# FFN2's operand sums taken from accumulating DMA to VectorE, in a kernel whose whole order is written out by hand

## The chip, the cores and the metric

The kernel runs on one core of a Trainium2 chip. The metric is device time in microseconds, as a median of several executions. A core has engines that work side by side, each through its own queue in order: TensorE (PE; its weight loads stand apart as PEld), VectorE (DVE), ScalarE (ACT), GpSimd (POOL) and SyncE (SP). DMA transfers are issued by POOL (its queue also casts and accumulates), SP and ACT.

## The reference, cut to what matters

```python
k_all = concat([beacon_k, k]); v_all = concat([beacon_v, v])      # 16 beacon rows, then S = 576
scores = scale * q @ k_all.T                                       # causal mask on the 576, none on the 16
a = softmax(scores); attn = a @ v_all                              # B = 8, H = 8, D = 64
x = attn as [4608, 512]
h = x @ w_in                                                       # 512 -> 2048
g = where(h > 0, h, exp(min(h, 0)) - 1)                            # ELU
out = g @ w_out                                                    # 2048 -> 512
```

## The kernel before, in words

Attention goes by batch b (0 to 7), each with two head groups of four; the two-layer feed-forward network goes by token tile t. Tiles 0 and 1 are two halves of the first 512 tokens, tiles 2 to 9 have 512 tokens each. The work of different batches and tiles is interleaved, so attention of a later batch fills engines while the network works on an earlier tile. Attention ends inside tile 7; tiles 8 and 9 run alone.

**The order is a list of words**, run from top to bottom by `run` (L825): `Q.6.0.7` calls step `Q` with 6, 0, 7. Each engine gets its instructions in the order of this list and does them in that order; between engines only data and buffers make anything wait. A last letter `v` puts a step on DVE that ACT does otherwise (`u`, `U`, `J`, `K`); `d`, in `Z` and `D`, made it an accumulating DMA. The steps that this text uses:

- `S`: scores of one column group on PE; `x`: their exponential on ACT; `m`: the causal mask on DVE; `D`: sums of exponentials on DVE; `L`, `W`: row sums and weighted values on PE; `n`, `M`: the normalisation.
- FFN1 of tiles 0 to 5: `F` on PE into one of the `hps` banks (pool of two), `e` (exponential, ACT), `u` (relu, ACT or DVE), `k` (DVE: joins them into the operand `gt`). `r` and `g` are another way of the same on DVE.
- FFN1 of tiles 6 to 9 is done by seven block products instead of eight: `X` and `H` make operand sums on DVE, `P` multiplies (4 matmuls), `K` copies a partial result (ACT, or DVE with `v`) or adds one (DVE), `E`, `U`, `V` are the exponential, the relu and the join.
- FFN2, also by seven products of blocks: `wt` makes the weight sums once, `Z.t.n` makes the operand's block sums for tile t, `Q.t.a.b` does matmuls a to b of the tile's 112, `J.t.p` takes a finished product out of PSUM (ACT, or DVE with `v`) and issues the store. Stores of tiles 3 to 8 accumulate in HBM.
- `lq`, `lk`, `lt`, `lp`, `lv`, `wi`, `wo`: loads; `lk`, `lv` and the weights are issued by POOL, the transposes `lt` by SP. `warm`: matmuls of zeros at the start.

`Z.t.n` works in place on the blocks A of `gt`: n = 3 writes A00 - A01 to its own tile `s3`; n = 1 adds A11 to A01; n = 2 makes A00 = A01 - A00; n = 4 takes A00 from A10. `B` is the whole tile, 0 or 1 a half (both only for tile 9). n = 2 reads what n = 1 wrote. The products of `Q` follow the order of `PH`: matmuls 0 to 31 read blocks before these sums, from 32 on those after n = 2, from 48 on n = 1's.

Of the six sums `Z.3.1` to `Z.8.1` the kernel before makes a DMA on POOL's queue (L571):

```python
nc.gpsimd.dma_start(out=o_, in_=b_, accum_op=op_)
```

All other `Z`, `H` and `wt` are a `tensor_tensor` on DVE (L573).

Of the kernel before, what the change touches and what calls it, by code (L numbers as in the profile page):

```python
# [12 lines left out]
ALU = mybir.AluOpType  # L13
# [4 lines left out]
def kernel(  # L18
# [107 lines left out]
    for b in range(BD):  # L126
        o_ = 0
# [62 lines left out]
    op = {}  # L190
# [378 lines left out]
    def sub(o_, a_, b_, op_=ALU.subtract, eng="v"):  # L569
        if eng == "d":  # L570
            nc.gpsimd.dma_start(out=o_, in_=b_, accum_op=op_)  # L571
            return
        (nc.vector if eng == "v" else nc.gpsimd).tensor_tensor(out=o_, in0=a_, in1=b_, op=op_)  # L573
# [258 lines left out]
    warm.1 lq.0.0.0.4 warm.1 warm.1 lq.0.1.0.4 warm.4 warm.1 lq.0.0.4.8 warm.1 warm.4 ident  # L832
    warm.1 bt bk T.0.0.0 cb.0.1 warm.1 cb.0.0 cb.0.2 warm.1 ck.0.0.0 lq.0.1.4.8 T.0.1.0 S.0.0.0
    T.0.0.1 cq.0.1.0 S.0.1.0 x.0.0.0 warm.1 cq.0.0.1 T.0.1.1 S.0.0.3 x.0.1.0 T.0.3.0 S.0.0.2
    cq.0.1.1 x.0.0.3 T.0.2.0 cq.0.3.0 lq.1.0.0.4 x.0.0.2 S.0.1.3 x.0.1.3 cb.0.3 warm.1 S.0.1.1
    x.0.1.1 T.0.2.1 S.0.1.2 tri cb.1.1 m.0.0.3 warm.1 x.0.1.2 S.0.3.0 cq.0.2.0 cq.0.2.1 T.0.3.1
    S.0.2.3 lv.0.2 warm.1 lv.0.0.1 x.0.3.0 m.0.3.0 m.0.0.0 x.0.2.3 S.0.2.0 m.0.1.0 x.0.2.0
    m.0.2.0 S.0.0.1 x.0.0.1 wi.2 S.0.2.2 x.0.2.2 L.0.A cb.1.0 T.1.0.0 cq.1.0.0 T.1.1.0 n.0.A
    cq.0.3.1 m.0.2.2 warm.4 S.0.2.1 W.0.A.0 ck.1.1.0 S.0.3.2 lv.0.3.4 x.0.2.1 m.0.1.2 x.0.3.2
    M.0.A.0 W.0.A.1 S.0.3.1 x.0.3.1 wi.1 m.0.2.3 M.0.A.1 S.1.1 cb.1.2 x.1.1 m.0.1.3 m.0.0.2  # L840
    S.0.3.3 F.0.4 x.0.3.3 m.0.3.3 S.1.4 x.1.4 m.0.3.2 e.0.4 L.0.B W.0.B.0 u.0.4.v k.0.4 n.0.B
# [145 lines left out]
```

## Time and profile before

| what | value |
|---|---|
| median of 3 runs | 325.75 us (325.48 to 327.68) |
| the profiled execution, its own time | 325.44 us |
| its span, first to last instruction | 323.7 us |
| PE, DVE, ACT, POOL busy | 97%, 90%, 90%, 36% |
| DMA software queue (POOL's), share of the 16 engines' time | 90.3% |
| the six accumulating DMAs | 512 KB each, 7.0 us to landing, POOL 9.9 us in all |

In the profile an engine's busy time is the union of its instructions' spans. Matmuls are pipelined, so a PE that is 97% busy is one that always has a matmul under way; it need not run at its peak rate. Idle time of an engine costs something only where another waits for what it does next.

### The profile page before, as it was taken

To read this page: it belongs to the slowest core of one execution; us is meant where nothing else is said; L and a number is where in the kernel's file an instruction comes from. 1 tells how busy PE (TensorE), PEld (TensorE's weight loads), DVE (VectorE), ACT (ScalarE), POOL (GpSimd) and SP (SyncE) were. 2 spreads that over 40 slices of the span, in tenths; PEclk is the share of its full clock that TensorE was granted. 3 is DMA by queue.
4 is the path that set the end of the run, shared out by engine and by line. 5 is a ranking of instruction groups with operands and counts; after the bars stand their busy time and mean duration, and the time that the engine had idled before them with its cause. 6 is when DMAs were issued, how large, how long until landed. Compare 5 with 4: busy or idle time off the path is not lost.

```text
span 323.7 us, 9046 instructions
## 1 busy us (share of the span) xinstructions
PE 315.3 (97%) x3705; PEld 224.0 (69%) x3708; DVE 291.9 (90%) x533; ACT 291.3 (90%) x485; POOL 116.1 (36%) x133
## 2 busy tenths in 40 slices
PE   8889999999999999999999999999999999999995
PEld 3557776656556656555655568788888888888884
DVE  2776999999979999989998999999999998989963
ACT  2998999999799999999999998999999999998930
POOL 8984729545247300550155061310401211131110
PEclk9999999999999999999999999999999999999999
DMA  9999999999999999599999992923484292374345
GB/s 113 179 186 204 185 201 165 159 139 172 141 171 174 174 140 177 68 132 148 195 134 136 166 116 62 146 53 93 61 141 99 35 130 59 90 111 73 97 99 130
DMA packets 141657, 42.53 MB, mean 131 GB/s; under 512 B 113200, under 2 KB 141616, under 8 KB 141616
## 3 DMA queue, kind: packets, MB, share of 16 engines
q0 software_dynamic: 106976, 26.35, 90.3%
q1 hardware_dynamic: 33920, 15.34, 24.9%
q8 instruction: 29, 0.48, 0.6%
q10 hardware_dynamic: 720, 0.26, 0.3%
q14 instruction: 12, 0.10, 0.1%
HBM read 37.22 MB, written 20.05 MB: 177 GB/s over the span
## 4 chain that ended last, share of the span: by engine, by line
PE 83%; ACT 8%; DVE 5%; issue 2%
PE ops L625 29%; PE hps L518 18%; PE hps L732 11%; PE sc L319 6%; PE ut L377 5%; ACT et L334 5%; PE sa L732 4%; PE sx L625 2%; PE w L205 2%; PE lt L377 1%; ACT e L528 1%; DVE gt L573 1%; PE lt L426 1%; DVE qkp L400 1%; PE ub L377 1%
## 5 line engine op out<-in xcount | busy, mean ns | idle before, releaser
L334 ACT ACTIVATE et<-sc 128x1024 f16<-128x1024 f32 (+2 forms) x114 | 104.1, 973 | 3.9 <-PE sc L319 3.5
L625 PEld LDWEIGHTS <-gt 128*128 128x128 f16 x864 | 83.2, 98 | 16.3 <-issue 1.3
L518 PE MATMUL hps<-xT,w_in 128*128 128x512 f16 (+1 forms) x384 | 79.1, 345 | 0.6 <-ACT e L528 0.4
L656 POOL DMA_DIRECT2D out_dram<-osb x18 | 22.0, 1224 | 127.1 <-ACT osb L649 65.8
L518 PEld LDWEIGHTS <-w_in 128*128 128x128 f16 x384 | 34.5, 98 | 28.8 <-issue 5.4
L625 PE MATMUL ops<-w_out,gt 128*128 128x256 f16 x416 | 54.1, 273 | 0.0
L625 PE MATMUL ops<-wt,gt 128*128 128x256 f16 x400 | 52.4, 273 | 0.0
L528 ACT ACTIVATE e<-hps 128x512 f32<-128x512 f32 x80 | 48.6, 625 | 2.1 <-PE hps L518 2.1
L548 DVE SCALAR_TENSOR_TENSOR gt<-e,r 128x512 f16<-128x512 f32 x73 | 48.8, 684 | 1.7 <-ACT e L528 0.8
L777 DVE SCALAR_TENSOR_TENSOR gt<-e,r 128x512 f16<-128x512 f32 x64 | 42.6, 683 | 1.9 <-ACT e L760 1.5
L149 POOL DMA_DIRECT2D v<-in_v_dram x40 | 38.6, 1270 | 7.8 <-issue 4.4
L534 ACT ACTIVATE r<-hps 128x512 f16<-128x512 f32 x55 | 33.1, 627 | 1.4 <-PE hps L518 1.4
L339 DVE TENSOR_TENSOR et<-et,triu 128x1024 f16<-128x1024 f16 (+5 forms) x66 | 26.5, 447 | 2.1 <-ACT et L334 2.1
L760 ACT ACTIVATE e<-qst 128x512 f32<-128x512 f32 x40 | 26.0, 657 | 1.5 <-DVE qst L749 1.5
L732 PEld LDWEIGHTS <-w_in 128*128 128x128 f16 x256 | 24.4, 98 | 4.2 <-issue 0.4
L573 DVE TENSOR_TENSOR gt<-gt 128x2048 f16<-128x2048 f16 (+1 forms) x24 | 25.9, 1084 | 0.2
L377 PEld LDWEIGHTS <-v 128*32 128x32 f16 (+1 forms) x800 | 17.5, 97 | 9.0 <-issue 1.4
L749 DVE TENSOR_TENSOR qst<-hps,kst 128x512 f32<-128x512 f32 x32 | 21.7, 684 | 0.7 <-ACT kst L746 0.6
L377 PE MATMUL ut<-et,v 128*32 128x464 f16 (+3 forms) x560 | 20.9, 296 | 0.1
L571 POOL DMA_DIRECT2D gt<-gt x6 | 9.9, 1658 | 27.2 <-DVE gt L548 20.2
L746 ACT COPY kst<-hps 128x512 f32<-128x512 f32 x32 | 18.7, 603 | 1.1 <-PE hps L732 1.1
L400 DVE TENSOR_TENSOR qkp<-qkp,et 128x1344 f16<-128x1344 f16 (+2 forms) x33 | 19.2, 583 | 0.4
(129 smaller groups left out, 539.2 us busy)
## 6 DMA issues: line engine op xcount, KB each, us to landing
out_dram<-sm SPq DMA_DIRECT2D x18, 256.0 KB, 2.7
out_dram<-osb POOLq DMA_DIRECT2D x18, 256.0 KB, 4.3
out_dram<-osb SPq DMA_DIRECT2D x17, 256.0 KB, 5.2
v<-in_v_dram POOLq DMA_DIRECT2D x24, 128.0 KB, 10.5
gt<-gt POOLq DMA_DIRECT2D x6, 512.0 KB, 7.0
scr<-in_q_dram POOLq DMA_DIRECT2D x5, 576.0 KB, 19.8
scr<-in_k_dram POOLq DMA_DIRECT2D x5, 576.0 KB, 21.4
w_in<-in_moe_w_in_dram POOLq DMA_DIRECT2D x8, 256.0 KB, 8.6
```

The lines of the kernel that those rows point to most:

```text
L149: nc.gpsimd.dma_start(out=vt[b][r0:r0 + n, j, :, :], in_=v[b, :, ilo[j]:ilo[j] + n, :].rearrange("h s d -> s h d"),)
L334: nc.scalar.activation(out=ets[b, d][:, :, a - EC2 * d:e - EC2 * d], in_=sc[b, g][:, :, a - c0:e - c0], func=AFT.Exp, bias=0.0, scale=SCALE)
L339: nc.vector.tensor_tensor(out=o, in0=o, in1=i, op=ALU.mult)
L377: nc.tensor.matmul(out=t[32 * i:32 * (i + 1), a - qa:e - qa], lhsT=ones[0:kc[j], :] if half is None else v16[0:kc[j], j, h, half:D:2], rhs ...
L518: nc.tensor.matmul(out=h[:, n_, :], lhsT=w_in16[:, cc, P * fc:P * (fc + 1)], rhs=xt[k][:, cc, a - TT * k:e - TT * k], start=(cc == 0), sto ...
L528: nc.scalar.activation(out=eb[t, i], in_=flat(hp[t, i]), func=AFT.Exp, bias=0.0, scale=1.0)
L534: nc.scalar.activation(out=rb[t, i], in_=flat(hp[t, i]), func=AFT.Relu, bias=0.0, scale=1.0)
L548: nc.vector.scalar_tensor_tensor(out=half(t, i), in0=eb[t, i], scalar=1.0, in1=rb[t, i], op0=ALU.subtract, op1=ALU.min)
L573: (nc.vector if eng == "v" else nc.gpsimd).tensor_tensor(out=o_, in0=a_, in1=b_, op=op_)
L625: nc.tensor.matmul(out=half_of(xy[t, n_], qd), lhsT=lw[:, P * qd:P * (qd + 1)], rhs=wt_[:, c, :], start=(first and c == 0 and (qd == 0 or ...
L732: nc.tensor.matmul(out=hx[t, g, n_][:, c, :], lhsT=lw, rhs=rh, start=(first and c == 0 and k_ == 0), stop=(k_ == 1), skip_group_check=True)
L777: eng.scalar_tensor_tensor(out=o_, in0=v_(eb[t, g, ph]), scalar=1.0, in1=v_(rb[t, g, ph]), op0=ALU.subtract, op1=ALU.min)
```

## The change: what it does

The choice of a DMA goes from `sub` and from `D`, so every `Z` is an instruction on DVE. The list of words is another one, of 1,502 words as before: six `Z.t.1.B.d` are now `Z.t.1.B`, some `u`, `U`, `J`, `K` have their `v` at other places (`u` 18 to 23 on DVE, `U` 24 to 16, `J` 9 to 8, `K` 2 to 4), seven `r` and `g` pairs stand at other places of tiles 2 to 5, one copy of batch 1's queries and keys goes to ACT in place of another, and nearly all words stand elsewhere.

```diff
     @step
-    def D_(b, d, n, eng="v"):
+    def D_(b, d, n):
...
-        if eng == "d":
-            nc.gpsimd.dma_start(out=o, in_=t[0:rows, :, col:col + e - a], accum_op=ALU.add)
-            return
...
     def sub(o_, a_, b_, op_=ALU.subtract, eng="v"):
-        if eng == "d":
-            nc.gpsimd.dma_start(out=o_, in_=b_, accum_op=op_)
-            return
         (nc.vector if eng == "v" else nc.gpsimd).tensor_tensor(out=o_, in0=a_, in1=b_, op=op_)
...
-            op[f](*[a if a in "ABRpvsd" else int(a) for a in args])
+            op[f](*[a if a in "ABRpvs" else int(a) for a in args])
...
     run("""
-    warm.1 lq.0.0.0.4 warm.1 warm.1 lq.0.1.0.4 warm.4 warm.1 lq.0.0.4.8 warm.1 warm.4 ident
+    warm.1 lq.0.0.0.4 warm.1 warm.4 warm.1 warm.1 warm.4 warm.1 lq.0.1.0.4 ident bt warm.1 bk
...
```

What the new list does to the engines' queues, at three places. First DVE at the block sums of tile 6 (`s_86<-gt` is `Z.6.3`, `gt<-gt` a `Z` in place; `qst_87<-hps,kst_88` is a `K` that adds, `gt<-e,r` a `V`, `r<-qst_87` a `U`, `qkp` a `D`, `et` a mask). Before:

```order
L573 TENSOR_TENSOR s_86<-gt 128x2048
L749 TENSOR_TENSOR qst_87<-hps,kst_88 128x512 x2
L339 TENSOR_TENSOR et<-et,triu 128x4x2x128
L339 TENSOR_TENSOR et<-et,triu 80x4x80
L400 TENSOR_TENSOR qkp<-qkp,et 128x4x336
L769 TENSOR_SCALAR r<-qst_87 128x512
L777 SCALAR_TENSOR_TENSOR gt<-e,r 128x2x256
```

and with the change:

```order
L743 TENSOR_TENSOR qst_87<-hps,kst_88 128x512
L771 SCALAR_TENSOR_TENSOR gt<-e,r 128x2x256
L743 TENSOR_TENSOR qst_87<-hps,kst_88 128x512
L567 TENSOR_TENSOR s_86<-gt 128x2048
L567 TENSOR_TENSOR gt<-gt 128x8x256 x2
L743 TENSOR_TENSOR qst_87<-hps,kst_88 128x512
L763 TENSOR_SCALAR r<-qst_87 128x512
```

`Z.6.1` now stands on DVE between `Z.6.3` and `Z.6.2`, and the three follow each other; before, `Z.6.2` stood 17 rows behind `Z.6.3`.

Second POOL, from the loads of batch 7's values on (`v_3580` before, `v_4006` with the change; `osb` are the accumulating stores of `J`). Before, where three more sums and ten more stores follow:

```order
L144 DMA v_3580<-in_beacon_v_dram 16x8x64
L149 DMA v_3580<-in_v_dram 112x8x64
L149 DMA v_3580<-in_v_dram 128x8x64 x3
L149 DMA v_3580<-in_v_dram 80x8x64
L656 DMA out_dram<-osb 128x2x256
L571 DMA gt<-gt 128x8x256
L656 DMA out_dram<-osb 128x2x256 x3
```

and with the change:

```order
L144 DMA v_4006<-in_beacon_v_dram 16x8x64
L149 DMA v_4006<-in_v_dram 112x8x64
L149 DMA v_4006<-in_v_dram 128x8x64 x3
L149 DMA v_4006<-in_v_dram 80x8x64
L650 DMA out_dram<-osb 128x2x256 x12
```

The sums are gone from this queue, and the last twelve stores follow each other with nothing between them.

Third DVE at the end of tile 9's FFN1 (`s_86<-gt 128x1024` and `gt<-gt 128x4x256` are half block sums; `sa` is another bank that `P` fills). Before:

```order
L749 TENSOR_TENSOR qst_87<-sa,kst_88 128x512
L777 SCALAR_TENSOR_TENSOR gt<-e,r 128x2x256 x2
L769 TENSOR_SCALAR r<-qst_87 128x512
L573 TENSOR_TENSOR s_86<-gt 128x1024
L573 TENSOR_TENSOR gt<-gt 128x4x256
L777 SCALAR_TENSOR_TENSOR gt<-e,r 128x2x256 x2
L573 TENSOR_TENSOR s_86<-gt 128x1024
L777 SCALAR_TENSOR_TENSOR gt<-e,r 128x2x256
L573 TENSOR_TENSOR gt<-gt 128x4x256 x3
```

and with the change:

```order
L743 TENSOR_TENSOR qst_87<-sa,kst_88 128x512
L771 SCALAR_TENSOR_TENSOR gt<-e,r 128x2x256
L567 TENSOR_TENSOR s_86<-gt 128x1024
L567 TENSOR_TENSOR gt<-gt 128x4x256
L771 SCALAR_TENSOR_TENSOR gt<-e,r 128x2x256 x2
L567 TENSOR_TENSOR s_86<-gt 128x1024
L771 SCALAR_TENSOR_TENSOR gt<-e,r 128x2x256 x2
L567 TENSOR_TENSOR gt<-gt 128x4x256 x4
```

One more join stands behind the second `s_86`, and four half sums follow in place of three.

More of the change, by code (lines that the diff above doesn't have):

```diff
@@ L836 @@
[L836 to L841, printed above, removed]
@@ new lines @@
+    x.0.1.1 lq.1.0.0.4 cb.1.0 cb.0.3 m.0.0.2 S.0.1.3 T.0.3.1 m.0.1.0 x.0.1.2 lv.0.0.1 m.0.1.2
+    lv.0.2 x.0.1.3 cq.0.2.1 S.0.3.0 x.0.3.0 wi.2 warm.1 cb.1.1 m.0.3.0 warm.1 S.0.0.3 x.0.0.3
+    S.0.2.0 S.0.2.3 cq.0.3.1 warm.1 x.0.2.0 m.0.2.0 S.0.3.2 lv.0.3.4 x.0.2.3 L.0.A T.1.1.0
+    x.0.3.2 cq.1.1.0 m.0.1.3 T.1.0.0 warm.4 S.0.3.3 n.0.A W.0.A.1 ck.1.0.0 m.0.2.3 S.0.2.2
+    x.0.3.3 M.0.A.1 x.0.2.2 W.0.A.0 m.0.3.2 S.0.3.1 x.0.3.1 m.0.3.3 wi.1 S.1.4 S.0.2.1 x.1.4
+    m.0.0.3 M.0.A.0 F.0.4 x.0.2.1 S.1.1 x.1.1 m.0.2.2 L.0.B e.0.4 n.0.B W.0.B.0 S.1.3 u.0.4.v
@@ new lines @@
+    F.3.0 Q.2.49.56 S.3.12 S.4.8 J.2.2.v g.3.10 F.3.9 e.3.0 u.3.0 lt.5.0 x.4.8 Q.2.63.70 Z.2.4.B
+    k.3.14 x.3.12 u.3.9.v m.4.0.1 e.3.9 m.3.1.1 D.3.1.1 F.3.4 S.4.4 S.4.1 k.3.9 e.3.4 x.4.4
+    F.3.12 x.4.1 Q.2.70.77 lt.5.1 e.3.12 W.3.1 J.2.3 D.3.1.2 D.3.1.3 L.3.1 u.3.4.v r.3.12
+    Q.2.77.84 g.3.12 n.3.1 Q.2.84.91 k.3.4 F.3.1 e.3.1 J.2.4 M.3.1.0 m.4.0.0 M.3.1.1 F.3.11
+    u.3.1 Q.2.91.98 e.3.11 S.5.4 u.3.11 x.5.4 S.4.7 F.4.3 x.4.7 k.3.1 Q.2.98.105 u.4.3 F.4.2
+    D.4.0.0 D.4.0.1 k.3.11 S.5.3 D.4.0.2 e.4.3 k.3.0 S.4.9 e.4.2 Q.2.105.112 x.5.3 x.4.9 J.2.5
@@ new lines @@
+    F.3.15 u.3.15 D.4.0.3 k.4.3 lk.6.0 lt.6.0 L.4.0 r.4.2 g.4.2 Z.3.3.B W.4.0 n.4.0 e.3.15
+    lk.7.0 M.4.0.1 F.4.7 M.4.0.0 u.4.7 e.4.7 k.3.15 F.4.11 e.4.11 S.5.7 S.5.2 x.5.2 J.2.6
+    u.4.11.v F.4.9 H.4.2 Q.3.0.7 u.4.9 k.4.7 x.5.7 F.4.8 Q.3.7.14 Z.3.1.B k.4.11 e.4.9 e.4.8
+    S.5.6 u.4.8.v x.5.6 k.4.9 S.4.12 F.4.14 F.4.12 e.4.14 H.2.0 Q.3.14.21 u.4.14.v x.4.12 e.4.12
+    S.5.1 S.4.10 x.5.1 x.4.10 F.4.10 J.3.0.v Q.3.21.28 S.4.11 r.4.12 S.5.11 g.4.12 e.4.10
+    Z.3.2.B r.4.10 F.4.6 x.4.11 Q.3.28.35 g.4.10 e.4.6 Q.3.35.42 S.5.9 m.4.1.0 r.4.6 k.4.14
@@ new lines @@
+    g.4.6 x.5.11 D.4.1.0 x.5.9 lt.6.1 J.3.1 S.5.0 x.5.0 k.4.8 F.4.4 e.4.4 Q.3.42.49 m.4.1.1
+    D.4.1.1 D.4.1.2 Q.3.56.63 S.5.10 D.4.1.3 u.4.4 m.5.0.0 S.5.5 x.5.10 F.4.15 x.5.5 m.5.1.0
+    u.4.15 e.4.15 F.4.1 lp.6.1 Z.3.4.B e.4.1 k.4.15 L.4.1 W.4.1 n.4.1 J.3.2 F.4.13 M.4.1.0
+    Q.3.49.56 M.4.1.1 u.4.1 lp.6.0 Q.3.63.70 S.6.2 S.6.4 e.4.13 k.4.1 F.4.5 x.6.2 m.5.0.1
+    Q.3.70.77 x.6.4 u.4.13.v J.3.3 lv.5 k.4.13 u.4.5.v D.5.0.0 D.5.0.1 S.5.12 S.5.8 x.5.12 lv.6
+    k.4.4 x.5.8 Q.3.77.84 Q.3.84.91 J.3.4 F.4.0 S.6.1 S.6.0 e.4.5 e.4.0 D.5.0.2 k.4.5 u.4.0
@@ new lines @@
+    D.5.0.3 x.6.1 x.6.0 Q.3.91.98 F.5.14 e.5.14 k.4.0 Z.4.3.B u.5.14.v F.5.12 L.5.0 e.5.12
+    Q.3.98.105 u.5.12 Q.3.105.112 lk.7.1 Z.4.1.B D.5.1.0 J.3.5 lt.7.0 F.5.13 F.5.10 n.5.0
+    M.5.0.0 S.6.3 e.5.13 k.5.14 u.5.13 W.5.0 x.6.3 e.5.10 u.5.10 k.5.13 S.6.5 F.5.6 F.5.15
+    m.5.1.1 x.6.5 M.5.0.1 e.5.6 S.6.9 k.5.10 u.5.6 D.5.1.1 e.5.15 H.4.0 m.6.0.0 u.5.15 S.6.6
+    x.6.6 D.5.1.2 x.6.9 D.5.1.3 F.5.7 k.5.6 k.5.15 F.5.5 W.5.1 L.5.1 u.5.7 J.3.6 Q.4.0.7
+    Q.4.7.14 u.5.5 k.5.12 m.6.0.1 Q.4.14.21 e.5.7 D.6.0.0 e.5.5 k.5.5 F.5.0 k.5.7 n.5.1 J.4.0
@@ new lines @@
+    H.1.3 F.5.8 M.5.1.0 M.5.1.1 u.5.0 Q.4.21.28 X.6.1 X.6.3 u.5.8 Z.4.2.B S.6.11 e.5.0 S.6.7
+    F.5.11 e.5.8 D.6.0.1 k.5.0 x.6.7 F.5.9 x.6.11 D.6.0.2 Q.4.28.35 S.6.12 e.5.9 S.6.8 X.6.2
+    u.5.11.v k.5.8 J.4.1 u.5.9 x.6.12 Q.4.35.42 Z.4.4.B e.5.11 F.5.1 Q.4.42.49 x.6.8 lp.7.0
+    e.5.1 u.5.1 F.5.2 lp.7.1 k.5.11 S.7.0 H.3.2 D.6.0.3 u.5.2 m.6.1.1 H.3.1 e.5.2 k.5.9 S.6.10
+    x.6.10 F.5.3 x.7.0 H.2.3 F.5.4 W.6.0 k.5.2 u.5.4 J.4.2 e.5.4 L.6.0 u.5.3 Q.4.56.63 m.6.1.0
+    H.3.0 e.5.3 P.6.0.0 K.6.0.0 n.6.0 Q.4.49.56 P.6.0.1 D.6.1.0 k.5.3 P.6.0.2 k.5.1 K.6.0.2
@@ new lines @@
+    P.9.1.3 E.9.0.1 J.7.6 K.9.1.0 K.9.1.3 E.9.0.5 Q.8.14.21 P.9.1.2 V.9.0.1 Z.8.1.B P.9.1.1
+    K.9.1.2 P.9.0.6 J.8.0 P.9.1.4 V.9.0.4 Z.8.2.B U.9.0.5 P.9.1.5 U.9.0.6 U.9.1.1 Q.8.21.28
+    K.9.1.5 Q.8.28.35 E.9.0.6 K.9.1.4 J.8.1 P.9.2.3 P.9.2.0 E.9.1.1 K.9.2.3 V.9.0.5 U.9.1.5
+    K.9.2.0.v Q.8.35.42 P.9.1.6 P.9.2.5 E.9.1.4 V.9.0.6 U.9.1.6 V.9.1.1 E.9.1.6 Q.8.42.49
+    P.9.2.1 P.9.2.2 Q.8.56.63 U.9.1.4.v P.9.3.0 J.8.2 E.9.1.5 K.9.2.2 Z.8.4.B V.9.1.4 K.9.2.5
+    Q.8.49.56 P.9.2.4 U.9.2.1 Q.8.63.70 E.9.2.1 V.9.1.5 V.9.2.1 K.9.3.0.v U.9.2.5 P.9.3.3
```

201 lines of the change are left out of this document (82 added, 119 removed).

## The prediction

> **What bounds the kernel now.** I read the page's first two parts and its chain first.
>
> ```profile
> span 323.7 us, 9046 instructions
> PE 315.3 (97%) x3705; PEld 224.0 (69%) x3708; DVE 291.9 (90%) x533; ACT 291.3 (90%) x485; POOL 116.1 (36%) x133
> ...
> PE   8889999999999999999999999999999999999995
> ...
> DVE  2776999999979999989998999999999998989963
> ACT  2998999999799999999999998999999999998930
> ...
> DMA  9999999999999999599999992923484292374345
> ...
> PE 83%; ACT 8%; DVE 5%; issue 2%
> ```
>
> PE sets the end: 83% of the chain is its, and from the fourth slice on it is full. But DVE and ACT are nearly full beside it, so a load that is put on DVE has little room. POOL, from which the change takes work, is idle for two thirds of the span.
>
> Next, how often PE itself waits: the two longest rows of that view, and those on `gt`, which `k`, `V` and `Z` write.
>
> ```profile
> PE sc L319 <- ACT et L334: 1.3, 4, 0.4
> PE w L205 <- DVE lo L172: 1.3, 1, 1.3
> ...
> PE hps L518 <- DVE gt L560: 0.2, 1, 0.2
> ...
> PEld L625 <- DVE gt L573: 0.2, 1, 0.2
> ```
>
> PE hardly waits for anyone, so there is little for a better order to win back. The one place with visible idle time is the start.
>
> To see where room is left, I cut the span at four PE steps whose start the chain and the timeline show, `Q.1.0.7`, `P.6.0.0`, `P.9.0.0` and `Q.9.0.7`:
>
> ```profile
> 59.83 1.20 PE ops L625 x10
> 193.12 0.61 PE L732 MATMUL hps<-xT,w_in 128*128 128x256 f16 x4
> 279.98 0.60 PE L732 MATMUL sa<-xT,w_in 128*128 128x256 f16 x4
> 307.67 0.38 PE L625 MATMUL sx<-w_out,gt 128*128 128x256 f16 x2
> ```
>
> and asked for the busy time of each engine between them (columns: stretch, its length, then PE, PEld, DVE, ACT, POOL with their instructions):
>
> ```profile
> 0.00:59.80 59.80, 55.34 (x958) 35.99 (x962) 45.91 (x104) 50.19 (x72) 41.73 (x63) 1.00 1.51 175
> 59.80:193.10 133.30, 133.13 (x1458) 79.42 (x1454) 127.49 (x222) 128.58 (x203) 51.67 (x53) 1.00 1.62 149
> 193.10:280.00 86.90, 86.90 (x942) 73.47 (x935) 84.82 (x154) 84.75 (x158) 15.26 (x12) 1.00 0.54 91
> 280.00:307.70 27.70, 27.50 (x252) 24.34 (x250) 25.80 (x44) 24.81 (x49) 6.25 (x5) 1.00 0.52 87
> ```
>
> The rest of the span, 16.0 us, is tile 9's FFN2. DVE's idle time is 13.9, 5.8, 2.1 and 1.9 us in the four stages; ACT's is 9.6, 4.7, 2.2 and 2.9. These are the rooms into which the change can put work at no cost.
>
> **What the removed DMAs were worth.**
>
> ```profile
> gt<-gt POOLq DMA_DIRECT2D x6, 512.0 KB, 7.0
> ...
> POOL gt L571 <- DVE gt L548: 20.2, 1, 20.2
> L571 POOL DMA_DIRECT2D gt<-gt x6: 1532/1562/2164, 133.4 to 285.6; - x6
> ...
> who waited for it (us, times):
> ```
>
> Each sum took 7.0 us to land, but the last row is empty in the profile: nobody waited for one. Taking them away therefore wins nothing on the path. It frees some 10 us of POOL (six of 1.6) and 3 MB of transfers from 133 to 292 us; POOL is no bound there, and I take nothing for that. The bounds are 0 and a gain of 0.2 us, what PE's weight load waits for a sum above.
>
> **What is put on DVE.** Rows for the durations (count, then busy us and mean ns):
>
> ```profile
> L573 DVE TENSOR_TENSOR gt<-gt 128x2048 f16<-128x2048 f16 x18 | 21.9, 1217 | 0.0
> L573 DVE TENSOR_TENSOR gt<-gt 128x1024 f16<-128x1024 f16 x6 | 4.0, 686 | 0.1
> L749 DVE TENSOR_TENSOR qst<-hps,kst 128x512 f32<-128x512 f32 x32 | 21.7, 684 | 0.7 <-ACT kst L746 0.6
> L777 DVE SCALAR_TENSOR_TENSOR gt<-e,r 128x512 f16<-128x512 f32 x64 | 42.6, 683 | 1.9 <-ACT e L760 1.5
> L769 DVE TENSOR_SCALAR r<-qst 128x512 f16<-128x512 f32 x22 | 9.0, 426 | 0.1
> L642 DVE COPY sm<-ops 128x512 f32<-128x512 f32 x4 | 2.7, 683 | 2.2 <-PE ops L625 2.2
> L706 DVE TENSOR_TENSOR qst<-xT 128x512 f16<-128x512 f16 x8 | 3.3, 417 | 0.0
> L573 DVE TENSOR_TENSOR w_in<-w_in 128x256 f16<-128x256 f16 x8 | 1.9, 280 | 0.0
> ```
>
> Six sums of 1.217 us are 7.3 us. The timeline shows that an instruction on DVE starts before the last has ended:
>
> ```profile
> 97.84 1.22 DVE L573 TENSOR_TENSOR gt<-gt 128x2048 f16<-128x2048 f16 x1
> 98.97 0.68 DVE L548 SCALAR_TENSOR_TENSOR gt<-e,r 128x512 f16<-128x512 f32 x1
> ```
>
> 98.97 - 97.84 is 1.13 us, so what a sum really takes from DVE's queue is 1.13, and six take 6.8. [...]
>
> Now stage by stage. In the list of words the PE steps ahead of `Q.1.0.7` are the same 95 in both kernels, and between the other cuts they are the same too (196, 154, 48, 16). So PE's work in each stage is unchanged, and I compare only what DVE and ACT have to do in the same stages.
>
> **Start to `Q.1.0.7`.** The list puts two more `e` and one more `x` on ACT here, and one `Z` (1.13) and two `wt` (0.69 each) on DVE. ACT is what runs without a break at the start:
>
> ```profile
> 8.85:59.80 50.95, 47.76 (x916) 32.79 (x918) 43.19 (x93) 48.32 (x70) 34.11 (x48) 1.00 1.60 185
> ...
> 102.43 0.60 ACT L528 ACTIVATE e<-hps 128x512 f32<-128x512 f32 x1
> 102.92 1.02 ACT L334 ACTIVATE et<-sc 128x1024 f16<-128x1024 f32 x1
> 103.83 0.60 ACT L534 ACTIVATE r<-hps 128x512 f16<-128x512 f32 x1
> ```
>
> From the first exponential (8.85) on ACT is idle for 50.95 - 48.32 = 2.6 us. By the starts above an `e` takes 0.49 and an `x` 0.91, so 2 x 0.49 + 0.91 = 1.9 us are added to an engine with 2.6 us of room, all of it waits of the sort that a new order need not remove. The cost lies between 0 (all in the room) and 1.9; I take 1.9, since ACT's row is 95% full and its idle pieces are waits for PE. On the other side, PE is idle 4.5 us of this stage, so a luckier start could gain; I bound that by 2.
>
> **`Q.1.0.7` to `P.6.0.0`.** `Z.3.1` and `Z.4.1` come here, but one `Z` has gone to the stage before; DVE gets one `Z`, five `u` (about a `K`'s 0.68 each) and three `H` (two of 0.28 each), and loses two `k`, two `wt`, four `J` copies and one `X`: 1.2 + 3.4 + 1.7 - 1.4 - 1.4 - 2.7 - 0.4 = +0.4, against 5.8 of room. ACT loses two `e`, five `u` and an `x` and gets four copies, by the starts above 7 x 0.49 + 0.91 - 4 x 0.49 = 2.4 us less. I take 0; the bounds are 0 and 0.4.
>
> **`P.6.0.0` to `P.9.0.0`.** DVE gets three `Z` (3.65), two copies (1.37) and two `k` (1.37), and loses one `V` (0.68), two `K` that add (1.37), one `U` from PSUM (0.68) and two from SBUF (0.85), one `X` (0.42) and three `H` (1.68): 6.39 - 5.68 = +0.7, against 2.1 of room. It would fit if all idle time could be used, and costs 0.7 where none can. What stands behind matters too: at tile 6 three sums now follow each other, some 3.5 us, and behind them the `K` that empties one of two `hps` banks, which PE's `P` waits for. PE has `Q.6.21.28` and a `P` or two meanwhile. I take 0.5 here; the ends are 0 and 3.5 (one such block uncovered).
>
> **`P.9.0.0` to `Q.9.0.7`.** This stage decides most. `Z.8.1` becomes DVE's, and the new list has more of tile 8's and 9's rest in here: one `Z` (1.22), one half sum (0.69), two `K` that add (1.37), two `V` (1.37), two `X` (0.83) and one copy (0.68), less one `U` from PSUM (0.68) and four from SBUF (1.70): 6.16 - 2.38 = +3.8, against 1.9 of room. ACT gets two `E` and six `U` and loses two copies, 6 x 0.49 = 2.9 us against 2.9. PE's 27.5 us of work can't cover a DVE that now has 25.8 + 3.8 = 29.6 us in a stage of 27.7: the stage grows by 1.9. Ends: 0 (work done ahead of the cut) and 3.8 (no room used).
>
> **The sum.** The tail behind `Q.9.0.7` keeps its matmuls: 0. So 1.9 + 0 + 0.5 + 1.9 = 4.3 on the profiled execution's 325.44 us (span 323.7 and 1.74 around it): **329.7 us**. That execution is 0.3 below the median of 325.75, so the forecast is 1.2% over the median. A measurement of this kernel can tell about 1% from no change, that is 322.5 to 329.0.
>
> **The rivals.**
>
> *The new order absorbs it.* All of the added 7 us fits the rooms, 13.9 + 5.8 + 2.1 + 1.9 us, because the list was laid out with the sums on DVE; PE, with the same steps, ends as before. For it: PE's waits are tiny, and over the whole span DVE stays below PE. Against: the last two stages have 4.0 us of room for 4.5 of work. It gives 325.4 plus up to 2: 325.4 to 327.5.
>
> *A shorter start, faster than before.* If the new order of loads and scores brings FFN1's first matmuls earlier, some of PE's 4.5 idle us of the first stage goes. The place is the stretch up to 59.8 us; the price is 2 of 4.5, giving 323.4, and it decides if ACT reaches its share of the first stage 2 us sooner. A gain over 1% needs 3 of the 4.5. Against: the first stage's ACT work is longer, not shorter.
>
> *DVE is the bound everywhere.* Then each of the added microseconds shows, about 7: 325.4 + 6.8 to 7.3 = 332.5. For it: DVE's digits are 9 nearly throughout. Against: 5.8 us of room in the second stage. [...]
>
> *Blocks of sums stall PE.* As at tile 6, the `hps` banks wait behind consecutive sums; with 2 us uncovered at tiles 4 to 8 that is 10 us: 335.5. Against: 34 sums stand in DVE's queue before, and PE's weight loads waited 0.2 us for one of them.
>
> **How the numbers follow.** Forecast 0.46 (own range 328 to 332, of which 0.40 over 329.0), absorbed 0.26, shorter start 0.11 (0.09 past 322.5), DVE everywhere 0.11, blocks 0.06. Slower by over 1%: 0.40 + 0.11 + 0.06 = 0.57; faster 0.09; within 0.34. The range of 8 in 10 runs from 323.8, which leaves out most of the shorter start, to 334.5, which takes in DVE as the bound and leaves out the blocks.
>
> **What the profile after would show.** PE's step `Q.1.0.7` near 61.7 instead of 59.8; the stretch to `P.6.0.0` still 133 us; the one from `P.9.0.0` to `Q.9.0.7` near 29.6 instead of 27.7, with DVE without a gap in it; 40 L567 sums and no accumulating `gt<-gt`; PE's waits on DVE rows of a few tenths. I am wrong if the first stage ends at or before 59.8, or if the stage of tile 9 keeps its 27.7 us: then the rooms took the work. Waits of PE over 1 us on `K` rows behind sums would speak for the blocks.

## The result and the profile after

| | before | after |
|---|---|---|
| median, 19 runs each | 325.88 us | 329.23 us |
| lowest and highest | 325.41, 327.87 | 327.34, 330.92 |
| span of the profiled execution | 323.7 us | 327.6 us |

The ratio is 1.0085 (95% interval 1.0068 to 1.0102): the changed kernel is 0.85% slower. That is half a microsecond from the 329.7 of the forecast, yet the profile shows that nearly none of it lies where the forecast put it. The interval leaves out no change, but not the 1% that the forecast's likeliest case went past. The ratio is taken over all runs; the two medians by themselves are 1.03% apart.

The page of the changed kernel, the rows that answer to those of before:

```profile
span 327.6 us, 9056 instructions
PE 317.7 (97%) x3708; PEld 224.2 (68%) x3708; DVE 297.4 (91%) x538; ACT 291.5 (89%) x486; POOL 116.3 (35%) x127
...
PEclk9999999999999999999999979999999999999999
...
PE 86%; ACT 5%; DVE 5%; POOL 2%; issue 1%; DVEq 0%; ACTq 0%
```

Two things are new: a slice in which the granted clock fell to 7 tenths, and POOL in the chain. DVE is 5.5 us busier, all sums being its own now: 24 rows of full sums on `gt` where there were 18.

```profile
L567 DVE TENSOR_TENSOR gt<-gt 128x2048 f16<-128x2048 f16 x24 | 29.2, 1217 | 0.3
```

PE's own waits (total, times, longest, in us), the first three rows:

```profile
PE sc L319 <- POOL qst L812: 2.5, 1, 2.5
PE sc L319 <- ACT et L334: 1.5, 5, 0.4
PE w L205 <- DVE lo L172: 1.3, 1, 1.3
```

One wait is new, and it is for POOL. Cut at the same PE steps as before, `Q.1.0.7`, `P.6.0.0`, `P.9.0.0` and `Q.9.0.7` (columns: stretch, length, then PE, PEld, DVE, ACT, POOL busy, granted clock):

```profile
0.00:59.60 59.60, 55.96 (x961) 35.99 (x962) 45.16 (x103) 50.39 (x73) 41.04 (x60) 1.00 1.51 175
59.60:197.20 137.60, 135.08 (x1456) 79.73 (x1455) 130.71 (x231) 128.07 (x202) 53.91 (x47) 0.99 1.38 131
197.20:284.20 87.00, 86.90 (x935) 73.21 (x933) 85.64 (x147) 84.45 (x157) 16.13 (x16) 1.00 0.49 83
284.20:311.50 27.30, 27.30 (x252) 24.39 (x250) 26.28 (x43) 26.82 (x53) 4.07 (x5) 1.00 0.37 70
311.50:327.60 16.10, 12.46 (x115) 10.93 (x112) 9.59 (x18) 1.77 (x5) 1.12 (x1) 1.00 0.49 114
```

By the exact starts of these steps the second stage grew from 133.35 to 137.70 us, by 4.3; the others are within 0.5 of before. So all of the loss stands in the one stage that was forecast at nothing. The timeline of that stage shows the place:

```profile
181.64 1.90 PE L515 MATMUL hps<-xT,w_in 128*128 128x512 f16 x8
...
185.12 1.19 POOL L650 DMA_DIRECT2D out_dram<-osb  x1 [16.39 <-ACT osb L643]
...
185.68 0.68 DVE L545 SCALAR_TENSOR_TENSOR gt<-e,r 128x512 f16<-128x512 f32 x1
185.85 4.80 POOL L812 COPY qst<-bkT 128x32 bf16<-128x32 bf16 x1
...
186.28 1.21 DVE L567 TENSOR_TENSOR gt<-gt 128x2048 f16<-128x2048 f16 x1
...
189.90 0.68 DVE L545 SCALAR_TENSOR_TENSOR gt<-e,r 128x512 f16<-128x512 f32 x1
190.59 0.20 POOL L812 COPY kst<-bkT 128x32 bf16<-128x32 bf16 x1
...
190.70 0.39 PE L319 MATMUL sc<-qst 64*128 64x512 bf16 x2 [2.49 <-POOL qst L812]
...
191.24 3.45 PE L515 MATMUL hps<-xT,w_in 128*128 128x512 f16 x8
...
191.35 0.49 DVE L567 TENSOR_TENSOR kst<-qst,w_in 128x256 f16<-128x256 f16 x2 [0.77 <-PE sc L319]
```

`lp.7.0` is a POOL copy of batch 7's beacon keys into the operand of its scores. In the new list it stands behind the store `J.4.1`, for whose data POOL waits 16.4 us. Its row then lasts 4.80 us; the like copy of `lp.7.1` right behind it takes 0.20. (The copy's row begins at 185.85, while the store ahead of it still runs, to 186.31; so 4.3 of the 4.80 us are the copy's own.) In the kernel before, `lp.7.0` had been done 35 us earlier:

```profile
154.74 0.68 POOL L818 COPY qst<-bkT 128x32 bf16<-128x32 bf16 x1
```

In the changed kernel PE reaches the scores `S.7.0` and stands still for 2.49 us, and its next eight matmuls take 3.45 us where eight in a row took 1.90 at 181.64, the first row shown. The clock of the two stretches (granted clock is the third number from the end):

```profile
188.20:190.70 2.50, 0.01 (x1) 0.00 (x1) 2.38 (x8) 1.40 (x3) 2.50 (x2) 1.00 0.28 44
190.70:194.60 3.90, 3.90 (x14) 1.23 (x14) 2.15 (x6) 1.94 (x2) 0.09 (x1) 0.59 0.00 0
```

2.5 us of standing still and 3.9 x (1 - 0.59) = 1.6 us of slower clock are 4.1, and `P.6.0.0` starts 4.15 later than before (197.27 against 193.12).

### The profile page after: what moved, and what is told of

Read it like the earlier page. It is cut to its first block, busy times and chain, and to the rows that moved or that the text cites. A ratio compares the mean times of both kernels' runs of the same rounds, so it can differ in the third digit from the quotient of the medians.

```text
span 327.6 us, 9056 instructions
## 1 busy us (share of the span) xinstructions
PE 317.7 (97%) x3708; PEld 224.2 (68%) x3708; DVE 297.4 (91%) x538; ACT 291.5 (89%) x486; POOL 116.3 (35%) x127
## 4 chain that ended last, share of the span: by engine, by line
PE 86%; ACT 5%; DVE 5%; POOL 2%; issue 1%; DVEq 0%; ACTq 0%
PE ops L619 31%; PE hps L515 20%; PE hps L726 10%; PE sc L319 7%; PE ut L377 6%; PE sa L726 4%; ACT et L334 4%; PE sx L619 2%; PE w L205 2%; PE lt L377 2%; POOL qst L812 1%; DVE qkp L278 1%; PE lt L423 1%; PE ub L377 1%; DVE gt L545 1%
## 5 line engine op out<-in xcount | busy, mean ns | idle before, releaser
L334 ACT ACTIVATE et<-sc 128x1024 f16<-128x1024 f32 (+2 forms) x114 | 105.8, 978 | 5.9 <-PE sc L319 5.6
L515 PE MATMUL hps<-xT,w_in 128*128 128x512 f16 (+1 forms) x384 | 81.2, 349 | 0.1
L619 PE MATMUL ops<-wt,gt 128*128 128x256 f16 x400 | 53.2, 273 | 0.0
L149 POOL DMA_DIRECT2D v<-in_v_dram x40 | 37.0, 1085 | 3.9 <-DMA scr<-in_q_dram 0.9
L567 DVE TENSOR_TENSOR gt<-gt 128x2048 f16<-128x2048 f16 (+1 forms) x30 | 33.2, 1111 | 0.5
L531 ACT ACTIVATE r<-hps 128x512 f16<-128x512 f32 x50 | 31.1, 631 | 2.6 <-PE hps L515 2.5
L533 DVE TENSOR_SCALAR r<-hps 128x512 f16<-128x512 f32 x23 | 15.7, 683 | 3.9 <-ACT e L525 3.9
L740 ACT COPY kst<-hps 128x512 f32<-128x512 f32 x30 | 17.7, 608 | 1.1 <-issue 0.7
```

Source lines behind the costliest of these rows:

```text
L149: nc.gpsimd.dma_start(out=vt[b][r0:r0 + n, j, :, :], in_=v[b, :, ilo[j]:ilo[j] + n, :].rearrange("h s d -> s h d"),)
L334: nc.scalar.activation(out=ets[b, d][:, :, a - EC2 * d:e - EC2 * d], in_=sc[b, g][:, :, a - c0:e - c0], func=AFT.Exp, bias=0.0, scale=SCALE)
L515: nc.tensor.matmul(out=h[:, n_, :], lhsT=w_in16[:, cc, P * fc:P * (fc + 1)], rhs=xt[k][:, cc, a - TT * k:e - TT * k], start=(cc == 0), sto ...
L531: nc.scalar.activation(out=rb[t, i], in_=flat(hp[t, i]), func=AFT.Relu, bias=0.0, scale=1.0)
L619: nc.tensor.matmul(out=half_of(xy[t, n_], qd), lhsT=lw[:, P * qd:P * (qd + 1)], rhs=wt_[:, c, :], start=(first and c == 0 and (qd == 0 or ...
```

## The experiments

Two theories stand at the start. **Late copy**: the new order has room for the sums, and the loss is one POOL copy that is late and, beside DVE, slow. **Rooms**: the added DVE and ACT work costs its price anywhere, and the copy only shows where.

**The copy earlier** (`e1_copy_early`). The two words of batch 7's copies move ahead of the store `J.4.0`:

```diff
-... J.4.0 ... J.4.1 ... lp.7.0 ... lp.7.1 ...
+... lp.7.0 lp.7.1 J.4.0 ... J.4.1 ...
```

> The changed kernel with lp.7.0 and lp.7.1 (the beacon keys of batch 7, two POOL copies) moved ahead of J.4.0 and J.4.1 in the list, so that they no longer stand behind the store of J.4.1 on POOL. Theory one, the late copy: PE waited 2.5 us for this copy at 188 to 191 us and then ran at half clock for 3.4 us, which lost 1.7 more; both go, so about 329.2 - 4.2 = 325.0 us, and P.6.0.0 starts near 193.0 instead of 197.2. Theory two, the rooms of my prediction (DVE has too much to do since the sums are its own): DVE's work is unchanged, the wait comes back somewhere else, 328 to 330 us.

Measured: 325.3 us, ratio to before 0.9973 (0.9950 to 0.9995). The second stage is back at its length of before, with all sums on DVE:

```profile
59.60:193.10 133.50, 133.46 (x1456) 79.35 (x1455) 130.38 (x231) 127.14 (x202) 50.33 (x47) 1.00 1.42 134
```

So the rooms theory falls, and this version is a little faster than both kernels.

**A memset in its place** (`e2_memset`).

```diff
     def lp(b, x_):
...
+        if (b, x_) == (7, 0):
+            nc.gpsimd.memset(t[:, :, 1, 0:NB], 0.0)
+            return
```

> The changed kernel with the copy of lp.7.0 made a memset of the same 128x32 at the same place in the list (batch 7's beacon keys of two head pairs are zeros: a part of the computation is left out). The copy took 4.80 us where others of its size took 0.20 us, while DVE ran instructions with two operands in SBUF back to back. Theory one, a POOL instruction that reads SBUF is held out by such DVE instructions: a memset reads nothing, takes some 0.2 us from 185.9 on, is done before PE asks at 188.2, and the time is 325.0 us. Theory two, POOL is slow here for another reason (its place behind the store, a busy sequencer): the memset is as long, 329 us.

Measured: 324.97 us, 0.9968 (0.9951 to 0.9986). On POOL:

```profile
186.03 0.61 POOL L813 MEMSET qst<- 128x32 bf16 x1
186.09 7.78 POOL L815 COPY kst<-bkT 128x32 bf16<-128x32 bf16 x1
```

An instruction of the same size at the same place that writes but doesn't read is done in 0.61 us. The second copy, which PE needs later, now takes 7.78 us (7.2 from the end of the memset) in place of 0.20: PE no longer stands still, DVE gets its blocks, and the copy is held longer.

**One half of the change at a time** (`e3_sums_only`, `e4_order_only`). The order of before with the sums on DVE, and the new order with the sums by DMA:

```diff
-... Z.3.1.B.d ... Z.8.1.B.d ...
+... Z.3.1.B ... Z.8.1.B ...
```

> The kernel before with nothing changed but the six sums, made on DVE at the places of the list where the DMAs stood (PE, ACT and all other words as before). The rooms of my prediction: 6.8 us more on DVE against 4.0 us of room in the last two stages, some 1 to 4 us slower, 327 to 330 us. The late copy: the sums fit between, 325.5 to 326.8 us, and no copy on POOL holds PE.

> The changed kernel's order with the six sums made by accumulating DMA again (the other part alone). The late copy: lp.7.0 still stands behind the store of J.4.1 and DVE's work around 186 us holds no sum of this kind, so PE still waits there, 328 to 330 us. The rooms: DVE is relieved of 6.8 us, 325 to 326 us. A third way: a sum now takes 7 us to land where the order has its reader right behind it (Z.6.1 and Z.6.2), which costs up to 5 us for each such place, 335 to 345 us.

Measured: 332.15 us, 1.0185 (1.0146 to 1.0224), and 350.25 us, 1.0733 (1.0690 to 1.0776). Neither theory had the first one. In it PE has seven waits behind DVE and ACT rows of 0.4 to 1.2 us that weren't there, and three stages grow with their sums. The third and fourth:

```profile
PE hps L732 <- DVE qst L749: 1.6, 2, 0.9
...
PE hps L518 <- DVE gt L560: 1.2, 1, 1.2
PE sa L732 <- DVE qst L749: 1.1, 1, 1.1
...
195.40:285.40 90.00, 87.75 (x940) 73.29 (x933) 88.12 (x157) 85.01 (x157) 10.67 (x9) 1.00 0.36 71
285.40:314.30 28.90, 27.65 (x251) 24.32 (x250) 27.02 (x45) 24.95 (x49) 4.73 (x4) 1.00 0.32 65
```

The second stage got two sums, 2.3 us, and is 2.7 longer; the third got three, 3.4, and is 3.2 longer; the fourth got one, 1.1, and is 1.2 longer. The other time, 350.25, is past even the third of the ways expected, 335 to 345. In that kernel DVE waits for the DMAs, and PE for DVE behind it:

```profile
DVE gt L570 <- DMA gt<-gt: 19.8, 3, 7.4
...
PE ops L622 <- DVE gt L570: 9.7, 2, 5.5
PE hps L729 <- DVE qst L746: 5.9, 1, 5.9
```

In the new list the sums that read the DMAs of tiles 6, 7 and 8 stand 1 to 7 words behind them; each DMA takes 6.9 us to land (median of the six). The late copy shows here too: it takes 4.72 us, and PE waits 2.40 for it. The clock adds some 9 us: the mean granted clock of the profiled run is 0.973 over 347.8 us, and by the page it is at 6, 6 and 8 tenths in the slices from 243.5, 278.2 and 313.0 us on, in or right behind those with PE's three waits of 4.2 to 5.9 us. So each order suits its own way of making the sums.

**Is it the place of the sums or their load?** (`e10_sums_late`). In the order of before each sum moves from the place where its DMA was issued to right ahead of the sum that reads it.

```diff
-... Z.4.1.B ... M.5.1.1 Q.4.14.21 Z.4.2.B
+... M.5.1.1 Q.4.14.21 Z.4.1.B Z.4.2.B
```

> The kernel before with its six sums on DVE, as in the run that gave 332.2 us, but each sum moved from where the DMA stood (6 to 68 words ahead of the sum that reads it) to the place right ahead of that reader. Theory of load (in the old order DVE has no idle time that the sums could use, wherever they stand): 331 to 333 us. Rival of the place (the sums stood too early, in front of DVE work that PE wanted soon, such as the adds of partial results that free the hps banks): 326 to 328.5 us, with the waits of PE for the adds L749 (0.9, 0.8 and 1.1 us) gone.

Measured: 332.34 us, 1.0198 (1.0158 to 1.0237), the time of the theory of load. PE's waits only change their name, from the adds L749 to the sums:

```profile
PE ops L625 <- DVE gt L573: 3.5, 5, 0.8
```

**No sums at all, in each order** (`e8_before_no_sums`, `e9_early_no_sums`).

```diff
-... Z.3.1.B.d ... Z.8.1.B.d ...
+...
```

> The kernel before without its six accumulating DMAs (the block sums Z.3.1 to Z.8.1 are left out, so FFN2 of tiles 3 to 8 is computed from wrong operands; nothing else is changed). The prediction's term: nobody waited for them, so taking them away wins 0 to 0.2 us: 325.5 to 326.0 us. Rival (their 3 MB and 10 us of POOL held other transfers up): 324.5 us or less. Together with the run that has the sums on DVE in this order (332.2 us) it gives what the six sums cost there: 6.2 to 6.7 us by the first, more by the second.

> The kernel with the early copy, without the six sums Z.3.1 to Z.8.1 (left out, so FFN2 of tiles 3 to 8 is computed from wrong operands): 6.8 us less on DVE in the new order. Theory that the new order has room for them: PE is idle only at the start and in the tail of the kernel with the early copy (4.2 and 3.6 of 7.9 us), so nothing is left to win between, and the time is 324.7 to 325.5 us, within 0.5 of the kernel with the early copy (325.3). Rival (DVE sets the pace in this order too): 319 to 322 us.

Measured: 326.88 us, 1.0023 (1.0000 to 1.0045), and 325.03 us, 0.9971 (0.9949 to 0.9994). Without its DMAs the old order is not faster, so they cost nothing; its profile is 1.4 us late at `Q.1.0.7` and 2.4 at `Q.2.0.7` (98.68 against 96.23), ahead of the first DMA at 133 us, so what it is late by isn't theirs; from `Q.2.0.7` to its end it takes 227.8 us against 227.5 before. In the new order the six sums cost some 0.3 us by the medians (325.3 against 325.03) and nothing by the ratios (0.9973 and 0.9971), in the old one 332.15 - 326.88 = 5.3 to 332.15 - 325.72 = 6.4. The profile of the second kernel shows what the new list did for DVE apart from the sums (third and fourth stage):

```profile
193.10:279.90 86.80, 86.70 (x936) 73.36 (x933) 82.98 (x144) 85.00 (x158) 16.15 (x16) 1.00 0.50 85
279.90:307.10 27.20, 27.20 (x252) 24.36 (x250) 25.04 (x42) 26.68 (x53) 4.04 (x5) 1.00 0.37 70
```

DVE has 82.98 and 25.04 us of work here, against 84.82 and 25.80 in the kernel before, which had no such sums on DVE either. 1.8 and 0.8 us have gone from the two stages without room, and the tail has 1.8 more (9.70 against 7.9).

**What holds the copy.** Three theories of its 4.8 us: POOL is slow behind a store; only an idle DVE lets it through; or DVE holds it by instructions of a certain kind. A probe (`e6_probe`) puts a memset and a copy behind each of 18 stores in the kernel with the early copy:

```diff
+        nc.gpsimd.memset(bkT[:, 0:2, 0:16], 0.0)
+        nc.gpsimd.tensor_copy(out=bkT[:, 2:4, 0:16], in_=bkT[:, 2:4, 16:32])
```

> The kernel with the early copy, plus 18 pairs on POOL, each behind a store: a memset of 128x32 and a copy of 128x32, both in columns of the beacon keys that nobody reads any more. Nothing is left out. Theory of the lock: the memsets, which read nothing, take 0.2 to 0.6 us; the copies take 0.2 us where DVE has gaps or reads PSUM and up to several us where it runs instructions with two SBUF operands back to back; the time stays at 325.3 us, at most 327 where a store is held behind a copy. Rival (POOL is slow behind a store, whatever it does): memset and copy are long at the same places, or the copies are all alike.

Measured: 324.95 us, 0.9972 (0.9955 to 0.9990). The memset and the copy at two of the 18 places, the store at the first, and DVE's rows around the end of two copies:

```profile
184.90 1.20 POOL L650 DMA_DIRECT2D out_dram<-osb  x1 [14.90 <-ACT osb L643]
...
185.62 0.62 POOL L816 MEMSET bkT<- 128x32 bf16 x1
185.68 7.83 POOL L820 COPY bkT<-bkT 128x32 bf16<-128x32 bf16 x1
...
192.33 1.11 DVE L397 TENSOR_TENSOR qkp<-et 128x1856 f16<-128x1856 f16 x1
193.70 0.69 DVE L545 SCALAR_TENSOR_TENSOR gt<-e,r 128x512 f16<-128x512 f32 x1 [0.26 <-ACT e L525]
...
241.93 0.59 POOL L816 MEMSET bkT<- 128x32 bf16 x1
241.99 2.28 POOL L820 COPY bkT<-bkT 128x32 bf16<-128x32 bf16 x1
...
243.52 0.68 DVE L771 SCALAR_TENSOR_TENSOR gt<-e,r 128x512 f16<-128x512 f32 x1
...
244.12 0.68 DVE L743 TENSOR_TENSOR qst<-hps,kst 128x512 f32<-128x512 f32 x1
```

17 of the memsets take 0.59 to 0.78 us and end 0.1 to 0.3 us behind the store ahead of them; one took 1.60, behind a store of 2.23, and ends 0.14 behind that. The copies, at the same places, have rows of 0.68 to 7.83 us, which are 0.04 to 7.28 from the end of the memset ahead of them. So POOL isn't slow as such, and the store is not the reason. The longest copy has its turn at 186.24, when the memset ends, beside DVE work without a gap, 17 instructions with both operands in SBUF from 186.10 on, and ends 0.07 us after DVE's first gap opens at 193.44. Neither data nor a buffer makes POOL wait here, so those are not the only things that hold one engine up for another.

A busy DVE alone does not hold it, though: in the kernel before, two copies ran in the middle of a DVE copy out of PSUM and took 0.24 us each.

```profile
38.72 1.35 DVE L278 COPY qkp<-tp 128x1152 bf16<-128x1152 bf16 x1
...
38.84 0.24 POOL L818 COPY kst<-bkT 128x32 bf16<-128x32 bf16 x1
...
39.10 0.24 POOL L818 COPY qst<-bkT 128x32 bf16<-128x32 bf16 x1
```

So the third theory fits the rows. Beside DVE instructions with two operands in SBUF the memset, which only writes, is done in 0.62 us (185.62), and the copy, which reads SBUF, ends 7.28 us after its turn; beside DVE's copy out of PSUM such a copy takes 0.24. By what means DVE holds it isn't shown.

The profiles show where such a copy gets through. In the profiles before and after, around the probes shown above, and around the late copy in `e5_scores_late`, `e7_pe_busy`, `e11_psum_between` and `e12_scores_late_2`, ten copies of 128x32 were held past the end of at least one DVE instruction: one before, three after, two probes, and the late copy of each of the four. All ten ended 0.05 to 0.07 us behind a DVE instruction that was followed by a gap of 0.03 us or more (8 of them) or by an instruction with an operand in PSUM (2). The copy at 241.99 is one of the two: it ends at 244.27, 0.07 behind the row of 243.52, and the next row, from 244.12, reads `hps`, a bank of PSUM. A copy that was held only by the one instruction under way when its turn came could end behind that even where the next had two SBUF operands: in the changed kernel the copy of 99.68 ended 0.07 us behind DVE's sum of 99.51, and the next row reads `e` and `r`. Why some of those got through isn't shown.

**Does DVE's next gap free the copy?** (`e5_scores_late`, and the same kernel again as `e12_scores_late_2`). The scores that need the copy come later, so that PE has other work:

```diff
-... S.7.0 ... F.5.3 x.7.0 H.2.3 F.5.4
+... F.5.3 H.2.3 F.5.4 S.7.0 x.7.0
```

> The changed kernel, with only the scores S.7.0 and their exponential x.7.0 moved behind F.5.4, so that PE has two FFN1 blocks to do before it asks for the late copy. Theory of the lock (a POOL copy that reads SBUF gets through only when DVE leaves a gap between instructions with two SBUF operands): DVE now gets its blocks and does not run dry at 190.6 us, so the copy lasts longer than 4.8 us, up to the 7.8 that the second copy took in the memset kernel (to about 193.9 us), PE asks at about 191 and still waits 1.5 to 2.9 us; 327.5 to 329.5 us. Rival (the copy takes 4.8 us whatever DVE does, for instance because a store stands just ahead of it): it ends at 190.6, PE never waits, 325.0 to 325.8 us.

> The kernel with S.7.0 and x.7.0 behind F.5.4 once more, for a profile with an undisturbed start (the first profile of it was 5.8 us late before anything that was changed). Theory of the lock: the copy starts at 185.9 and takes 6.8 us, PE waits 2.0 us for it at 190.7 and again runs at a lower clock behind it; 328.8 to 329.3 us. Rival: 4.8 us for the copy, no wait.

Measured: 329.14 us, 1.0093 (1.0056 to 1.0129), and 327.84 in the single later run. From the second profile:

```profile
185.83 6.81 POOL L812 COPY qst<-bkT 128x32 bf16<-128x32 bf16 x1
...
192.70 0.39 PE L319 MATMUL sc<-qst 64*128 64x512 bf16 x2 [2.03 <-POOL qst L812]
...
192.70:196.00 3.30, 3.30 (x69) 2.23 (x69) 1.12 (x1) 2.87 (x6) 0.09 (x1) 1.00 0.03 5
```

The copy is held 2.0 us longer as the scores come later, as the theory of the lock had it. In the changed kernel the gap that freed it at 190.58 was DVE's wait for these scores, which PE couldn't start without the copy (the row at 191.35 above); here DVE goes on with other blocks. The later scores win nothing. The last row is a miss: the clock behind this wait stayed at 1.00, and the time is 1.0 below the expected range. In the first profile, behind a wait of the same 2.03 us, the clock did fall to 0.5.

**A piece of DVE work out of PSUM in the middle** (`e11_psum_between`).

```diff
-... e.5.1 u.5.1 F.5.2 lp.7.1 k.5.11 S.7.0
+... e.5.1 u.5.1.v F.5.2 lp.7.1 k.5.11 S.7.0
```

> The changed kernel with one word changed: u.5.1 becomes u.5.1.v, so the relu of one FFN1 block is made by DVE, out of PSUM (L533, 0.68 us, one operand, not in SBUF), right behind the block sum Z.4.4 and ahead of the join k.5.11, in the middle of the 4.8 us for which the late POOL copy was held. DVE gets 0.6 us more work, and never stands idle. Theory of the lock (only instructions with two SBUF operands hold the copy; one from PSUM lets it through): the copy ends beside that instruction, at about 187.5 us, after some 1.7 us in place of 4.80; PE waits for nothing, and the time is 325.3 to 326.3 us. Rival (any busy DVE shuts POOL out, and only its standing idle let the copy through): the copy lasts to 190.6 us or longer, 329 to 330 us.

Measured: 326.19 us, 1.0015 (0.9995 to 1.0034).

```profile
185.76 1.71 POOL L812 COPY qst<-bkT 128x32 bf16<-128x32 bf16 x1
...
188.08 0.69 DVE L533 TENSOR_SCALAR r<-hps 128x512 f16<-128x512 f32 x1 [0.68 <-ACT e L525]
```

The copy took the expected 1.71 us and PE didn't wait for it. But the relu itself had to wait 0.68 us for ACT, and the copy went through in that gap of DVE, at 187.47, ahead of the relu. So this run doesn't tell a PSUM operand from an idle DVE; it shows only that a gap frees the copy. Two new waits of PE, 0.15 us for the relu and 0.75 for an ACT exponential behind it, are what it is slower by than the early copy.

**What the standing still costs besides itself** (`e7_pe_busy`). Twelve more matmuls ahead of `S.7.0`, which fill PE's wait:

```diff
+                nc.tensor.matmul(
+                    out=h[:, 0, :], lhsT=w_in16[:, cc, P * i:P * (i + 1)],
+                    rhs=xt[k][:, cc, a - TT * k:e - TT * k], start=(cc == 0), stop=(cc == NCC - 1))
...
-... k.5.11 S.7.0
+... k.5.11 again.5.2.3 S.7.0
```

> The changed kernel with twelve more matmuls of 0.22 us (a block of F.5.2 done three times again into its own bank) right ahead of the scores that wait for the late copy: 2.6 us of work where PE stood idle for 2.5. Theory that the idle time costs 1.7 us more through the clock: the granted clock stays at 1.00 from 191 to 195 us, FFN1's matmuls there stay at about 0.23 us each, and the time is 327.2 to 327.9 us. Rival (the 4.05 us are wait and queue alone, the clock only goes with it): 329.0 to 329.6 us. If PE's waiting was what let DVE run dry, the copy takes longer than 4.8 us here and the time is 329 or more although the clock stays.

Measured: 327.66 us, 1.0057 (1.0042 to 1.0072): with 2.6 us of useless work in place of the wait the kernel is 1.6 us faster than the changed one, and the clock stays whole:

```profile
191.20:195.00 3.80, 3.80 (x59) 1.87 (x62) 2.28 (x6) 3.66 (x6) 0.08 (x1) 1.00 0.02 4
```

The copy takes 4.79 us, as in the changed kernel, although PE was busy: DVE still waited 0.81 us for the scores behind it. So it wasn't PE's idleness as such that gave DVE its gap.

## Why the prediction was right in its number and wrong in its steps

- **Start to `Q.1.0.7`, +1.9.** Measured -0.2 (59.57 against 59.77). ACT was to get 1.9 us more; in the stage it is busy 50.39 us against 50.19. By the forecast's own test ("I am wrong if the first stage ends at or before 59.8") this step fell. The mis-sized term is the count: I counted the rows that the list puts between two PE words and took them for work done between the two times. Each engine runs through the list at its own pace, and a row that stands behind the cut in one list can be done ahead of it.
- **`Q.1.0.7` to `P.6.0.0`, 0.** Measured +4.3, all of the loss. DVE did fit into the stage, as argued: with the early copy it has 130.38 us of work in 133.5. The step that failed is the sentence on POOL, "POOL is no bound there, and I take nothing for that". It judged POOL by its busy share and asked only for what goes from its queue. What the list moves past POOL's stores was not priced: the copy `lp.7.0`, which now stands behind a store whose data come late, and which PE needs.
- **`P.6.0.0` to `P.9.0.0`, +0.5.** Measured +0.2; DVE's +0.7 came as +0.8 and fitted. The three sums at tile 6 let no `P` wait.
- **`P.9.0.0` to `Q.9.0.7`, +1.9, the stage that "decides most".** Measured -0.4 (27.3). DVE's +3.8 was +0.5. Again the count by list places; with the first stage it made 3.8 of the forecast's 4.3. The second test of the forecast, a stage of tile 9 that keeps its 27.7, speaks against it too: the rooms took the work.
- **The removed DMAs, 0, and a sum's 1.13 us on DVE.** Right: the old order without them is not faster, and in that order the six cost 5.3 to 6.4 of the reckoned 6.8.
- **The rivals.** *The new order absorbs it* is what happened to the sums (some 0.3 us; 325.3 with the copy early, against its 325.4); only the copy keeps the changed kernel from it. *A shorter start* came to 0.2 of its 2 us. *DVE is the bound everywhere*, 332.5, is what the old order does with the sums (332.15, 332.34); I had weighed it for a kernel whose list is another. *Blocks of sums* shows there too, with three waits behind the adds L749 of 0.8 to 1.1 us, and not in the changed kernel.

That the number was near is luck, the sum of two errors: 4.3 us of costs that weren't there, and 4.3 us that I had not looked for. The length of the wait could not be read off the profile before: of its ten POOL copies of 128x32 nine take 0.14 to 0.48 us from the end of the POOL row ahead of them, and one 1.15. What could be read there is the place: the new list moved `lp.7.0` and `lp.7.1` from ahead of tile 4's stores to behind the first of them on POOL, `J.4.1`, whose data come late.

What stays open: which copies get through behind the one DVE instruction under way when their turn comes, and which waits of PE a lower clock follows.

## What to carry to other kernels

Price what a new order moves past each queue, the idle engines' too: ask for every instruction that the busy engine waits for, what now stands ahead of it, when that will be done, and what the other engines run beside it then. Count the duration of a row from the end of the row ahead of it on its queue. A load moved to a nearly full engine is free or costs its full price depending on the order around it (here some 0.3 us in the one, 5.3 to 6.4 in the other), so measure the two halves of such a change apart. Read work per stage from what an engine does in the time, not from where rows stand in a list.

## What the runs showed of the hardware

- A POOL copy of 128x32 that reads SBUF took 0.20 us with DVE idle (after, 190.59), 0.24 beside a DVE copy out of PSUM (before, 38.84 and 39.10), and up to 7.83 (7.28 from the end of the row ahead; `e6_probe`, 185.68) beside DVE work with two SBUF operands that left no gap. Of the 18 memsets of that size at the probes' places 17 took 0.59 to 0.78 us. The ten copies that were held past a DVE instruction's end, as counted above, all ended 0.05 to 0.07 us behind one that a gap (8) or an instruction with a PSUM operand (2) followed.
- A PE that stood still for 2.49 us ran the next 3.9 us at a mean granted clock of 0.59, 1.6 us lost on top of the wait. Of two waits of 2.03 us one had a lower clock behind it and one had not, and behind waits of 2.40 and 3.12 us it stayed, so the length alone doesn't decide:

| profile, PE's wait | granted clock behind it |
|---|---|
| after, 188.21 to 190.70 (2.49 us) | 0.50 from 191.44 to 194.85 |
| e5, 196.51 to 198.54 (2.03) | 0.57, 0.50, 0.50 and 0.72 in the four microseconds from 199 to 203 |
| e12, 190.67 to 192.70 (2.03) | 1.00 up to 202 |
| e4, 188.22 to 190.62 (2.40) | 1.00 up to 198 |
| e5, 44.00 to 47.12 (3.12) | 90% or more in both slices of the page from 41.7 to 58.3 |

What decides isn't shown. It differs from run to run: of the 19 runs of the changed kernel four, at 327.34 to 327.82 us, had a mean granted clock of 1.000, and the other fifteen, from 328.73 on, had 0.989 to 0.995 (0.995 over 327.6 us is 1.6 us). With PE kept busy (e7) all ten runs had 0.998 to 1.000.
